# Putting the row of maxima in place with five products and a copy instead of a transpose and a transfer, for the first twelve heads

## The chip, the cores and the metric

The kernel runs on one core of a Trainium2 chip. The metric is the device time of one execution in microseconds (us). The core has five engines with queues of their own: TensorE (PE in the profile; its weight loads are PEld), VectorE (DVE), ScalarE (ACT), GpSimd (POOL) and SyncE (SP). Transfers between memories go through 16 DMA engines; SP, POOL and ScalarE issue them.

## The reference

```python
# q, k, v: (8, 8, 576, 64)   batch, heads, sequence, head size
scores = (1 / 8) * q @ k.transpose(0, 1, 3, 2)
scores = where(pos_i // 64 >= pos_j // 64, scores, -1e9)   # causal in blocks of 64
scores = scores - scores.max(-1, keepdims=True)
attn = exp(scores)
attn = attn / (attn.sum(-1, keepdims=True) + 1e-9)
x = (attn @ v).transpose(0, 2, 1, 3).reshape(4608, 512)
h = x @ moe_w_in                                           # 512 x 2048
sp = maximum(h, 0) + log1p(exp(-abs(h)))
out = (h * erf(sp)) @ moe_w_out                            # 2048 x 512
```

An attention over 64 heads (8 batches of 8) is followed by a dense layer with a gate ("MoE" in the names). The factors of the inputs make the scores large, so that the maximum must be subtracted. The weights come in as 64-bit numbers.

## The kernel before, in words

**Heads.** The head number n runs from 0 to 63 in one loop. In turn n the program writes out together: the load of a later head (`load_qk`), the maxima of head n + 2 (`maxes`), the probabilities of head n (`probs`), the products with v of an earlier pair (`pv`), the normalising of a group of four heads (`normalise`), the conversion of raw weights (`conv`, `split_next`; lines 130 to 136 and 156 to 157) and steps of the dense layer (`moe1`). Each is a list of steps with a start and an end between 0 and 1, and `merge` interleaves the lists by these numbers. The Tile framework then plans the order in which each engine gets the instructions, from their costs, their dependencies and this order of writing. An engine works through its queue in order.

**A head's tile.** `qk_of(n)` is a tile of 128 partitions with four parts of 576 columns: `klh`, `qhl`, `kh`, `qh`. Partitions 0 to 63 of `kh` and `qh` hold the high part of k and q (float32 rounded to a shorter form), and `klh` and `qhl` hold residuals and copies with which the product becomes more exact. Five more partitions of `kh` and `qh`, 64 to 68 (`D` to `D + 4`, with D = 64), are extra rows of the product: four mask rows, which put a large negative number on the half of a diagonal block that is masked, and one row that is 1 in `kh` and the row of maxima, with its sign turned, in `qh`. The product over 69 partitions then gives scores with the mask and with the maximum subtracted. Before the change the mask rows stand on partitions 64 to 67 and the constant row with the maxima on 68.

**Where the tiles lie.** Heads below EARLY = 12 go round through six tiles (four `qk`, two `qke`), later heads through four (NB = 4, NE = 2). The two others become weight slots after head 12. The rows of `maskrows` are put into the six tiles once, at the start. Head n + 4 is loaded in turn n below 12, head n + 3 above 12: POOL issues two loads (lines 408 and 410, or 412 and 414), SP one (`st`), and later POOL computes the residuals (lines 417 and 420). Early heads get part of their copies from ScalarE (line 427).

**Maxima.** In `maxes(n)`, steps a to d multiply the queries of a head by its keys (line 444, tile `s`, over 68 partitions: q, k and the mask rows) and VectorE takes the negated maximum of each row of scores into a column of `mx`, 128 queries by five columns (line 447). Step e joins the last two columns (line 472). Then the maxima, which lie one per partition, must become one row of 576 numbers on one partition of `qh`. Before: one transpose of `mx[:, :5]` (line 474) gives five partitions of 128 numbers in PSUM, ScalarE copies them to `mt` (line 476), and a transfer issued on ScalarE's queue writes the five pieces one after the other to partition 68 (line 477).

**Probabilities.** `probs(n)` multiplies `kh` by `qh` over 69 partitions (line 490, tile `t`) and adds the residual product (line 491); ScalarE takes the exponential (line 495). The product of line 490 reads the row of maxima. The products with v are line 539 and the sums of rows line 562; for the first 24 heads both are in float32. `normalise` sends x to DRAM (`x_d`) through POOL (lines 626 and 627).

**PSUM.** `bank` gives out a PSUM bank for each product: before the dense layer has loaded its first x, seven banks in rotation, later four.

**Dense layer.** `moe1` multiplies x by w_in (line 201), applies the gate (lines 169 to 177, of which line 177, the residual `m_gl`, runs on POOL while heads are in work) and multiplies by w_out (line 210). It starts when the first batch of eight heads is normalised and the first weights are converted. After the last head only it is left.

Of the kernel before, what the change touches and what calls it, by code (L numbers as in the profile page):

```python
# [23 lines left out]
def f32(ap):  # L24
    return ap.bitcast(F32)
# [7 lines left out]
def tile_attention_moe(ctx: ExitStack, tc: tile.TileContext, qk, v, w, maskrows, selws, out):  # L33
    nc = tc.nc
    B, H, D4, S = qk.shape
    D = D4 // 4
    NT, DM = out.shape
    NF = w.shape[0]
    P = 128
# [22 lines left out]
    ident = cpool.tile([P, P], F32, name="ident")  # L62
# [3 lines left out]
    zeros = cpool.tile([P, 1], F32, name="zeros")  # L66
# [26 lines left out]
    EARLY = 12  # L93
    NE = 2
# [181 lines left out]
    NB = 4  # L276
# [3 lines left out]
    def qk_of(n):  # L280
        return qks[n % len(qks) if n < EARLY else n % NB]
# [28 lines left out]
    with tc.tile_pool(name="apool", bufs=2) as apool, tc.tile_pool(name="spool", bufs=1) as spool, \  # L310
# [6 lines left out]
        mxs = [spool.tile([P, 7], F32, name=f"mx{i}") for i in range(2)]  # L317
# [15 lines left out]
        def bank(name):  # L333

            turn.append(0)
            k = len(turn) % 8 if not loaded else 0
            if k in (2, 5):
                return ps_h.tile([P, 512], F32, tag="h", name=name)
            if k in (3,):
                return ps_o.tile([P, 512], F32, tag="o", name=name)  # L340
            return ps_a.tile([P, 512], F32, tag="a", name=name)
# [55 lines left out]
        def part(n, i):  # L397

            return qk_of(n)[:, i * S : (i + 1) * S]

        def load_qk(n):
            b, h = divmod(n, H)
            t = qk_of(n)[:, : 4 * S].rearrange("p (i n) -> p i n", n=S)
            st = apool.tile([P, S], F32, tag="st", name=f"st_{n}", bufs=2)

            def a():
                if n < COPIED:
                    nc.gpsimd.dma_start(t[:D, 2:4, :], qk[b, h, 2 * D :].rearrange("(s d) n -> d s n", d=D))
                    nc.sync.dma_start(st, qk[b, h, : 2 * D])
                    nc.gpsimd.dma_start(t[D:, 0, :], qk[b, h, :D])  # L410
                    return
                nc.gpsimd.dma_start(t[:D, 1:4, :], qk[b, h, D:].rearrange("(s d) n -> d s n", d=D))
                nc.sync.dma_start(st, qk[b, h, : 2 * D])
                nc.gpsimd.dma_start(t[D:, 0:2, :], qk[b, h, : 2 * D].rearrange("(s d) n -> d s n", d=D))

            def low_q():
                nc.gpsimd.tensor_tensor(out=t[D:, 1, :], in0=st[D:, :], in1=f32(t[D:, 1, :]), op=ALU.subtract)

            def c():
                nc.gpsimd.tensor_tensor(out=t[:D, 0, :], in0=st[:D, :], in1=f32(t[:D, 2, :]), op=ALU.subtract)  # L420
                if n >= COPIED:
                    low_q()

            def copies(mx):
                for r, src in ((slice(0, D), f32(t[:D, 3, :])), (slice(D, P), st[D:, :])):
                    nc.vector.tensor_copy(t[r, 1, :1][:1], mx[r, 0:1][:1])
                    nc.scalar.copy(t[r, 1, :], src)
                low_q()

            if n < COPIED:  # L430
                copied[n] = copies
            return a, c

        COPIED = EARLY
        copied = {}

        def maxes(n):

            mx, K = mxs[n % 2], D + 4
            kh, qh = part(n, 2), part(n, 3)  # L440

            def mm(dst, i, k0, w_):
                r = min(P, S - i * P)
                nc.tensor.matmul(dst[:r, :w_], lhsT=qh[:K, i * P : i * P + r], rhs=kh[:K, k0 : k0 + w_], start=True, stop=True)  # L444

            def red(col, src, r=P):
                nc.vector.tensor_reduce(out=mx[:r, col : col + 1], in_=src, axis=AX.X, op=ALU.max, negate=True)  # L447

            def a():
                s = bank(f"s01_{n}")  # L450
                mm(s, 0, 0, 256)
                mm(s[:, 256:], 1, 0, 256)
                red(0, s[:, :128])
                red(1, s[:, 256:])

            def b():
                s = bank(f"s2_{n}")
                mm(s, 2, 0, 384)
                red(2, s[:, :384])

            def c():
                s = bank(f"s3_{n}")
                mm(s, 3, 0, 512)
                red(3, s)

            def d(j):
                s = bank(f"s4_{n}_{j}")
                mm(s, 4, 288 * j, 288)
                red(5 + j, s[:64, :288], 64)

            def e():
                nc.vector.tensor_reduce(out=mx[:64, 4:5], in_=mx[:64, 5:7], axis=AX.X, op=ALU.min)
                pt = bank(f"mt{n}")
                nc.tensor.transpose(out=pt[:5, :P], in_=mx[:, :5], identity=ident)
                mt = apool.tile([5, P], F32R, tag="mt", name=f"mt_{n}")
                nc.scalar.copy(mt, pt[:5, :P])
                nc.scalar.dma_start(f32(qk_of(n)[D + 4 : D + 5, 3 * S : 4 * S + 64]).rearrange("o (i p) -> o i p", p=P), f32(mt))

            return [a, b, c, lambda: d(0), lambda: d(1), e]

# [173 lines left out]
        for n in range(2):  # L654
            *steps, rows[n] = maxes(n)
            for f in steps:
                f()
            copied.pop(n)(mxs[n])
            if n:
                copied.pop(2)(mxs[n])  # L660
            if n == 0:
                v32 = load_v(0, 0, mxs[0][:1, 3:4])
                rows.pop(0)()
            next_raw(mxs[n][:1, 3:4])
# [34 lines left out]
        for n in range(N + 3):  # L699
# [9 lines left out]
            if n + 2 < N:  # L709
                *steps, rows[n + 2] = maxes(n + 2)  # L710
                lists.append((late("max", steps), 0, 1))
# [16 lines left out]
            if n % 2 == 0 and 2 <= n <= N:  # L728
                j = n // 2 - 1
# [75 lines left out]
```

## Time and profile before

| | |
|---|---|
| time, median of 3 runs | 1230.59 us (1229.72 to 1231.5) |
| profiled execution | 1236.01 us, span 1234.2 us |
| TensorE busy | 1149.7 us, 93% of the span |
| VectorE, ScalarE busy | 825.6 us (67%), 863.8 us (70%) |
| POOL busy | 476.2 us (39%) |
| mean granted TensorE clock | 0.973 |
| bytes moved by DMA | 148.24 MB, mean 120 GB/s |

How to read it: the span is one execution between its first and its last instruction. A row of a group has line, engine, operation, the tile written <- the tiles read, shapes and count; behind the first bar the busy time and the mean of one in ns, behind the second the idle time of the engine just before these instructions and what ended it. In a timeline a row has start, duration, engine, line and operation, and in brackets the idle time before it with what ended it. A waits row has the waiting engine, tile and line <- what it waited for: us in total, times, longest. `qke` is one of the two tiles that exist only for the early heads. PEclk is the clock that TensorE was granted, as a share of the full one.

### The profile page before, as it was taken

To read this page: it belongs to the slowest core of one execution; us is meant where nothing else is said; L and a number is where in the kernel's file an instruction comes from. 1 tells how busy PE (TensorE), PEld (TensorE's weight loads), DVE (VectorE), ACT (ScalarE), POOL (GpSimd) and SP (SyncE) were. 2 spreads that over 40 slices of the span, in tenths; PEclk is the share of its full clock that TensorE was granted. 3 is DMA by queue.
4 is the path that set the end of the run, shared out by engine and by line. 5 is a ranking of instruction groups with operands and counts; after the bars stand their busy time and mean duration, and the time that the engine had idled before them with its cause. 6 is when DMAs were issued, how large, how long until landed. Compare 5 with 4: busy or idle time off the path is not lost.

```text
span 1234.2 us, 23125 instructions
## 1 busy us (share of the span) xinstructions
PE 1149.7 (93%) x8874; PEld 795.7 (64%) x8874; DVE 825.6 (67%) x1559; ACT 863.8 (70%) x1675; POOL 476.2 (39%) x459
## 2 busy tenths in 40 slices
PE   6878988889999999999999999999999999999996
PEld 3555655666666667767766676766766766666663
DVE  5888887795676767677668666666667644555454
ACT  3675866686676776777777776777867776766664
POOL 7556154534353434435454444435443312100000
PEclk9886999999998999999999999999999999999999
DMA  9796368544554445453453445444544121121202
GB/s 235 215 248 172 115 192 215 145 100 110 128 139 109 120 118 123 129 140 100 122 139 93 128 110 129 107 127 110 121 113 117 56 63 61 62 69 52 69 26 77
DMA packets 94111, 148.24 MB, mean 120 GB/s; under 512 B 7620, under 2 KB 44804, under 8 KB 94002
## 3 DMA queue, kind: packets, MB, share of 16 engines
q1 hardware_dynamic: 69696, 93.34, 25.0%
q0 software_dynamic: 23616, 53.15, 20.3%
q8 instruction: 70, 1.15, 0.4%
q10 hardware_dynamic: 690, 0.28, 0.1%
q14 instruction: 39, 0.32, 0.1%
HBM read 118.15 MB, written 28.31 MB: 119 GB/s over the span
## 4 chain that ended last, share of the span: by engine, by line
PE 34%; DVE 27%; ACT 26%; DMA 6%; issue 6%; POOL 1%; ACTq 0%; DVEq 0%; SPq 0%; POOLq 0%
PE m_h L201 11%; PE o L210 10%; DVE m_r L173 6%; DVE m_r L174 6%; DVE m_r L175 5%; PE u L539 5%; ACT m_r L170 4%; ACT m_r L169 4%; ACT m_r L172 4%; ACT m_r L171 4%; ACT m_gh L176 3%; DVE mx L447 3%; PE t L490 2%; PE s L444 2%; PE t L491 2%
## 5 line engine op out<-in xcount | busy, mean ns | idle before, releaser
L201 PE MATMUL m_h<-xh,w 128*128 128x256 f16 x1584 | 323.6, 274 | 7.9 <-DVE m_r L175 7.1
L201 PEld LDWEIGHTS <-w 128*128 128x128 f16 x2376 | 224.4, 98 | 97.3 <-issue 10.2
L177 POOL TENSOR_TENSOR m_gl<-m_r,m_gh 128x512 f16<-128x512 f32 x114 | 135.9, 1192 | 290.3 <-ACT m_gh L176 265.5
L210 PE MATMUL o<-w,m_gh 128*128 128x512 f16 x792 | 233.7, 383 | 1.1 <-DVE pt L252 1.1
L447 DVE TENSOR_REDUCE mx<-s 64x1 f32<-64x288 f32 (+4 forms) x384 | 173.7, 469 | 88.5 <-PE s L444 87.7
L173 DVE SCALAR_TENSOR_TENSOR m_r<-m_r,m_r 128x512 f32<-128x512 f32 x144 | 118.7, 824 | 168.8 <-ACT m_r L172 164.2
L176 ACT CAST m_gh<-m_r 128x512 f16<-128x512 f32 x144 | 88.8, 617 | 182.8 <-DVE m_r L175 181.8
L201 PE MATMUL m_h<-xl,w 128*128 128x256 f16 x792 | 216.7, 274 | 0.0
L495 ACT ACTIVATE p<-t 128x288 f32<-128x288 f32 (+4 forms) x384 | 143.4, 382 | 60.7 <-PE t L491 52.2
L490 PE MATMUL t<-qk 69*128 69x288 f32 (+1 forms) x360 | 158.6, 442 | 17.2 <-DMA qk<-mt 9.5
L444 PE MATMUL s<-qk 68*128 68x256 f32 (+2 forms) x360 | 141.2, 426 | 17.3 <-DMA qk<-qk 8.4
L201 PE MATMUL m_h<-xh,we 128*128 128x256 f16 x720 | 149.1, 276 | 6.1 <-DVE m_r L175 5.9
L210 PE MATMUL o<-w,m_gl 128*128 128x512 f16 x396 | 143.4, 385 | 0.0
L169 ACT ACTIVATE m_r<-m_h,c,bs 128x512 f32<-128x512 f32 (+3 forms) x192 | 123.9, 665 | 27.2 <-PE m_h L201 23.9
L210 PEld LDWEIGHTS <-m_gh 128*128 128x128 f16 x1152 | 100.7, 98 | 63.4 <-issue 9.6
L201 PEld LDWEIGHTS <-we 128*128 128x128 f16 x1080 | 102.6, 99 | 50.2 <-issue 9.4
L420 POOL TENSOR_TENSOR qk<-st,qk 64x576 fp32r<-64x576 f32 x60 | 87.3, 1455 | 107.4 <-DMA qk<-qk 89.3
L507 DVE TENSOR_TENSOR p<-p,p 128x832 f16<-128x832 f32 x80 | 81.5, 1019 | 65.8 <-ACT p L506 65.6
L174 DVE SCALAR_TENSOR_TENSOR m_r<-m_r 128x512 f32<-128x512 f32 x144 | 119.0, 826 | 3.2
L491 PE MATMUL t<-qk 128*128 128x288 f32 (+1 forms) x360 | 112.8, 314 | 0.0
L210 PE MATMUL o<-we,m_gh 128*128 128x512 f16 x360 | 103.8, 385 | 5.2 <-ACT m_gh L176 5.2
L171 ACT ACTIVATE m_r<-m_r,c 128x512 f32<-128x512 f32 x144 | 103.7, 720 | 2.7 <-ACT m_r L170 0.6
(141 smaller groups left out, 1953.0 us busy)
## 6 DMA issues: line engine op xcount, KB each, us to landing
qk<-qk POOLq DMA_DIRECT2D x52, 432.0 KB, 4.8
st<-qk SPq DMA_DIRECT2D x64, 288.0 KB
qk<-qk POOLq DMA_DIRECT2D x60, 288.0 KB, 4.9
raw<-w SPq DMA_DIRECT2D x32, 512.0 KB
v<-v SPq DMA_DIRECT2D x16, 640.0 KB
x_d<-xs POOLq DMA_DIRECT2D x32, 288.0 KB, 3.2
xh<-x_d SPq DMA_DIRECT2D x36, 256.0 KB
xl<-x_d SPq DMA_DIRECT2D x36, 256.0 KB
```

The source lines that it names most:

```text
L169: nc.scalar.activation(r0s[:, :, lo:hi], h[:, :, lo:hi], AF.Tanh, bias=const(p1), scale=bss[b][g][:, 0:1])
L171: nc.scalar.activation(r0, r1, AF.Square, bias=const(b2), scale=a2)
L173: nc.vector.scalar_tensor_tensor(out=r0, in0=r0, scalar=c4, in1=r1, op0=ALU.add, op1=ALU.mult)
L174: nc.vector.scalar_tensor_tensor(out=r0, in0=r0, scalar=c5, in1=r0, op0=ALU.add, op1=ALU.mult)
L177: (nc.gpsimd if lag[-1] == 3 else nc.vector).tensor_tensor(out=gl, in0=r0, in1=gh, op=ALU.subtract)
L201: nc.tensor.matmul(h[:, k, :], lhsT=wf[:, a, sl], rhs=x[:, cc, :], start=cc == 0 and i == 0, stop=cc == NCC - 1 and i == 2)
L210: nc.tensor.matmul(o[c], lhsT=a[:, sl], rhs=wf[:, b_, :], start=u == u0 and k == 0 and not lo and b_ == 2, stop=u == u1 - 1 and k == nu - ...
L444: nc.tensor.matmul(dst[:r, :w_], lhsT=qh[:K, i * P : i * P + r], rhs=kh[:K, k0 : k0 + w_], start=True, stop=True)
L447: nc.vector.tensor_reduce(out=mx[:r, col : col + 1], in_=src, axis=AX.X, op=ALU.max, negate=True)
L490: nc.tensor.matmul(s[:kk, :w_], lhsT=kh[:K, ks], rhs=qh[:K, q0 : q0 + w_], start=True, stop=False)
L491: nc.tensor.matmul(s[:kk, :w_], lhsT=klh[:, ks], rhs=qhl[:, q0 : q0 + w_], start=False, stop=True)
L495: nc.scalar.activation(p32s[part][:kk, c : c + w_ - skip], s[:kk, skip:w_], AF.Exp, scale=SCALE)
```

## The change

For heads below 12, step e of `maxes` makes five products with the identity instead of one transpose. Each has one column of `mx` as its stationary operand and writes 128 numbers to partition 64 of a PSUM bank: four into one bank, the fifth into a second. ScalarE copies the first 512 numbers and then the last 64 from there straight into `qh`, on the same partition 64. The transfer is gone for these heads. For later heads the transpose, the copy and the transfer stay; only the partition written to is now 64.

For this the rows change places: the constant row and the row of maxima move to partition 64, the mask rows to 65 to 68. The products for the maxima (line 444) must read the mask rows, so they now read 69 partitions, and the row of maxima of the head that had the tile before would be in them. So, from the seventh head on (n >= 6), POOL writes zeros to partition 64 of `qh` before it issues the head's loads.

```diff
@@ load_qk
             def a():
+                if n >= NB + NE:
+                    nc.gpsimd.tensor_copy(t[D : D + 1, 3, :], zeros[D : D + 1].broadcast_to([1, S]))
                 if n < COPIED:
@@ maxes
-            mx, K = mxs[n % 2], D + 4
+            mx, K = mxs[n % 2], D + 5
...
             def e():
                 nc.vector.tensor_reduce(out=mx[:64, 4:5], in_=mx[:64, 5:7], axis=AX.X, op=ALU.min)
+                if n < EARLY:
+                    for c, w_ in ((0, 4), (4, 1)):
+                        pt = bank(f"mt{n}_{c}")
+                        for i in range(w_):
+                            nc.tensor.matmul(pt[D : D + 1, i * P : (i + 1) * P], lhsT=mx[:, c + i : c + i + 1], rhs=ident, start=True, stop=True)
+                        q0, q1 = c * P, min(S, (c + w_) * P)
+                        nc.scalar.copy(qh[D : D + 1, q0:q1], pt[D : D + 1, : q1 - q0])
+                    return
                 pt = bank(f"mt{n}")
                 nc.tensor.transpose(out=pt[:5, :P], in_=mx[:, :5], identity=ident)
                 mt = apool.tile([5, P], F32R, tag="mt", name=f"mt_{n}")
                 nc.scalar.copy(mt, pt[:5, :P])
-                nc.scalar.dma_start(f32(qk_of(n)[D + 4 : D + 5, 3 * S : 4 * S + 64]).rearrange("o (i p) -> o i p", p=P), f32(mt))
+                nc.scalar.dma_start(f32(qk_of(n)[D : D + 1, 3 * S : 4 * S + 64]).rearrange("o (i p) -> o i p", p=P), f32(mt))
@@ kernel
     for j in range(4):
-        maskrows[j, 1, 128 * j : 128 * j + 64] = -(2.0**100)
-        maskrows[j, 0, 128 * j + 64 : 128 * j + 128] = 1.0
-    maskrows[4, 0] = 1.0
+        maskrows[j + 1, 1, 128 * j : 128 * j + 64] = -(2.0**100)
+        maskrows[j + 1, 0, 128 * j + 64 : 128 * j + 128] = 1.0
+    maskrows[0, 0] = 1.0
```

## The prediction

> **What bounds the kernel now.** I read the page's head and its forty slices first, to see which engine is full in which stage.
>
> ```profile
> span 1234.2 us, 23125 instructions
> PE 1149.7 (93%) x8874; PEld 795.7 (64%) x8874; DVE 825.6 (67%) x1559; ACT 863.8 (70%) x1675; POOL 476.2 (39%) x459
> PE   6878988889999999999999999999999999999996
> PEclk9886999999998999999999999999999999999999
> ```
>
> TensorE is 93% busy over the whole, and from the sixth slice on nearly full at an almost full clock. Only the first four or five slices of 30.9 us have holes and a low clock. The twelve heads that the change names lie there, so I cut that stage into tens of microseconds.
>
> ```profile
> core 0: us, PE busy (x) PEld busy (x) DVE busy (x) ACT busy (x) POOL busy (x), PEclk, DMA share, GB/s
> 20.00:30.00 10.00, 6.67 (x33) 5.09 (x34) 6.33 (x17) 6.35 (x17) 5.31 (x6) 0.88 0.91 281
> 30.00:40.00 10.00, 9.13 (x48) 6.07 (x47) 5.63 (x14) 6.66 (x15) 7.62 (x7) 0.60 0.91 246
> 40.00:50.00 10.00, 8.11 (x67) 5.70 (x66) 9.80 (x25) 7.24 (x22) 6.79 (x7) 1.00 0.54 139
> 60.00:70.00 10.00, 8.02 (x57) 5.73 (x48) 9.74 (x26) 8.10 (x22) 4.89 (x5) 0.84 0.93 240
> 80.00:90.00 10.00, 5.85 (x44) 3.83 (x37) 7.42 (x22) 8.38 (x23) 4.41 (x5) 0.96 0.90 248
> 90.00:100.00 10.00, 10.00 (x75) 6.62 (x73) 4.92 (x10) 4.38 (x11) 4.38 (x4) 0.70 0.83 167
> ```
>
> No single engine holds this stage. From 20 to 40 us the DMA engines are full (share 0.91); from 40 to 80 VectorE is (9.80 and 9.74 of 10); from 80 to 100 neither is: TensorE first sits idle, then works at a clock of 0.70. Next: what TensorE waits for up to 130 us, and where.
>
> ```profile
> PE t L490 <- DMA qk<-mt: 9.5, 6, 3.1
> PE t L490 <- DMA qke<-mt: 1.1, 1, 1.1
> ...
> 27.12 0.37 PE L490 MATMUL t<-qk 69*128 69x288 f32 x1 [3.08 <-DMA qk<-mt]
> ...
> 81.64 0.37 PE L490 MATMUL t<-qk 69*128 69x288 f32 x1 [1.02 <-DMA qk<-mt]
> 89.26 0.58 PE L490 MATMUL t<-qk 69*128 69x288 f32 x1 [3.13 <-DMA qk<-mt]
> ```
>
> The transfer of the row of maxima (`qk<-mt`) ends seven waits of TensorE, 10.6 us together, two of them over 3 us. The chain of work that ended last, cut to 12 to 130 us, tells which of them count.
>
> ```profile
> by line: PE u L539 12.6%; DMA qk<-mt 12.5%; DMA raw<-w 11.3%; DVE mx L447 8.0%; issue 6.7%; DVE w L133 5.7%; PE t L490 5.3%; DVE w L132 3.9%; PE s L444 3.6%; PE t L491 3.1%; ACT p L495 2.8%; DVE w L157 2.5%; DMA st<-qk 2.3%; ACT w L156 2.3%
> ...
> 13.18 6.93 DMA qk<-mt
> 31.72 6.86 DMA raw<-w
> 49.39 6.49 DMA raw<-w
> 77.86 3.64 DMA qk<-mt
> 84.93 4.20 DMA qk<-mt
> 90.98 4.88 PE u L539 x20
> 144.73 3.00 PE u L539 x28
> ```
>
> 12.5% of 118 us is 14.8 us: three transfers of the row (6.93, 3.64, 4.20). The 3.08 us wait before 27.12 is not among them: there the chain goes through the loads of raw weights. The last two rows are for the clock. The same products of line 539 took 4.88 us for twenty right after the 3.13 us hole, 244 ns each, and 3.00 us for twenty-eight later, 107 ns each.
>
> **The change part by part.** These are the groups whose durations I use:
>
> ```profile
> L474 PE MATMUL mt<-ident,mx x12: 272/274/421, 12.4 to 121.0; 128*5 128x128 f32 x12
> L474 PE MATMUL mt<-ident,mx x4: 272/274/275, 46.8 to 77.3; 128*5 128x128 f32 x4
> 148.07 0.27 PE L474 MATMUL mt<-ident,mx 128*5 128x128 f32 x1
> 148.18 0.59 PE L210 MATMUL o<-w,m_gh 128*128 128x512 f16 x2
> L539 PE MATMUL u<-p,v 128*64 128x128 f32 x48 | 6.1, 317 | 0.0
> L476 ACT CAST mt<-mt 5x128 fp32r<-5x128 f32 x64 | 15.8, 247 | 7.8 <-PE mt L474 7.0
> L477 ACTq DMA_DIRECT2D qk<-mt x9: 699/700/720, 13.2 to 135.9; - x9
> L176 ACT CAST m_gh<-m_r 128x512 f16<-128x512 f32 x144 | 88.8, 617 | 182.8 <-DVE m_r L175 181.8
> L495 ACT ACTIVATE p<-t 64x64 f32<-64x64 f32 x64 | 13.4, 209 | 11.9 <-PE t L491 10.7 <-PE s L444 0.8 <-ACT a L130 0.2
> L328 POOL CAST selw<-zeros x1: 613/613/613, 18.9 to 18.9; 128x512 fp32r<-128x512 f32 x1
> ```
>
> *Removed, in each of twelve heads:* one transpose, one ScalarE copy of 247 ns, one transfer. The transpose lasts 274 ns but holds TensorE for little: the next matmul started 0.11 us after it (148.07 to 148.18). The transfer's issue holds ScalarE's queue for up to 0.70 us.
>
> *Added on TensorE:* five plain f32 products of one column of maxima with the 128 columns of the identity. No row shows such a product alone. From below: 107 ns, the mean step of the f32 stream of line 539. From above: 317 ns, the full duration of a 128-column f32 product of line 539. I take 0.21, the middle, because the five follow each other, so their ends overlap, but they all go to one PSUM partition, so I do not expect them side by side as in that stream. Then a head costs 5 x 0.21 - 0.11 = 0.94 us more on TensorE (bounds 0.43 and 1.48), twelve heads 11.3 us (5 to 18).
>
> *Where this lies on the path:* the twelve transposes run from 12.4 to 121.0 us, four of them between 46.8 and 77.3. Up to 70 us the pace is set by loads and VectorE, and TensorE has the holes quoted; I cost the seven heads there at nothing. If that cover goes, they cost 6.6 us. Five heads (the one at 77.3 us and the four after it) run where the chain passes through TensorE: 5 x 0.94 = 4.7 us.
>
> *Added on ScalarE:* a copy of 1x512 and one of 1x64, by the rows of 128x512 (617 ns) and 64x64 (209 ns) 0.83 us, less the 0.25 of the old copy: +0.58 us a head. Against it the queue is free of a 0.70 us issue, so I cost it at nothing; bounds -0.1 and +0.58 us a head. A new wait comes with it: the second copy sits in ScalarE's queue until the fifth product is done, and the exponentials of line 495 and the weight conversions stand behind it. That is one product more, 0.2 to 0.3 us, which ScalarE's idle time (a sixth to a third in the windows above, up to 90 us) covers.
>
> *The row's latency:* instead of 3.6 to 6.9 us of transfer there are four more products (0.84) and about 0.6 us more of copying, some 1.4 us. The first product of `t` (288 columns) needs only the first copy.
>
> *What the removed waits give, one by one:*
> ```profile
> 19.87 0.68 ACT L130 ACTIVATE a<-raw 128x512 f32<-128x512 f32 x1 [2.71 <-DMA raw<-w]
> 21.71 0.68 DVE L132 SCALAR_TENSOR_TENSOR w<-a,w 128x512 int32<-128x512 int32 x1
> ```
> - The first (13.18 to 20.11): next on the chain is VectorE's weight conversion, begun at 21.71. It needs line 130, which began at 19.87 when its own load landed, so it can begin at 20.55: 1.2 us gained, not 6.9. Late next: the raw weights.
> - Before 27.12: not on the chain, but the clock was 0.60 in the ten microseconds from 30. I take 0.5; bounds 0, and 3.1 with 9.13 x 0.4 = 3.7 for the clock.
> - Before 81.64: 1.0 us.
> - Before 89.26: 3.1 us of idle. I keep all of it, since the extra products were charged above. And if the hole is short the clock stays up: twenty products at 107 instead of 244 ns save 2.7 us. Together 5.8.
> - The four small waits lie under a full VectorE or full DMA: nothing.
> Sum 8.5 us; at most 17.0 (10.6 of waits, 2.7 and 3.7 of clock).
>
> *Added on POOL:* from the seventh head on, a write of zeros on one partition of 576 elements ahead of the head's loads, 0.66 us by the 613 ns of 512 elements; 58 of them, 38 us on an engine that is 39% busy.
>
> ```profile
> L412 POOL DMA_DIRECT2D qk<-qk x52 | 33.4, 643 | 113.7 <-PE t L491 88.3 <-PE o L210 12.7 <-PE s L444 7.9
> PE s L444 <- DMA qk<-qk: 8.4, 3, 7.0
> L444 PE MATMUL s<-qk 68*128 68x256 f32 (+2 forms) x360 | 141.2, 426 | 17.3 <-DMA qk<-qk 8.4
> 300.00:400.00 100.00, 95.84 (x753) 66.74 (x753) 64.87 (x118) 66.91 (x129) 41.01 (x39) 0.97 0.48 120
> ```
>
> It waits for the matmuls that last read this slot, as the load behind it does already (88.3 us). Queued behind it are two load issues, the residuals of lines 420 and 417, MoE's subtraction of line 177, and the x residuals. All come up to 0.66 us later. The second row counts TensorE's waits for loads of q and k up to 130 us, 8.4 us in three places, and the third, over the whole span, has no more. I cost it at nothing; bounds: 0, and 0.66 us for each of 52 late heads, 34 us, if the loads became the pace. In the steady stage TensorE has four percent idle (95.84 of 100), which no part of the change touches.
>
> *Moved:* the row of maxima and the constant row exchange places with the mask rows, and the maxima's matmul reads 69 rows instead of 68. The shape of its moving columns stays: nothing. One PSUM bank more is drawn for each early head, from seven in rotation: within the range.
>
> *The sum:* 8.5 - 4.7 = 3.8 us. The profiled execution took 1236.0 us, span 1234.2; the median of the runs is 1230.6, so this execution is 0.4% long, and I take the difference off the median: 1226.8.
>
> **A rule against it.** The Trainium skill, "TensorE: Matmul & The Clock Gate", section Terms, says that the transpose mode is four times faster for FP32. By that rule a plain product steps at 4 x 0.11 = 0.44 us, which is the price of the second rival below. The trace has no lone plain f32 product to settle it; the stream of line 539 (107 ns) speaks against it, but its products may run side by side.
>
> **The rivals.** About 0.2%, 2.5 us, is what a measurement of this kernel can tell from no change.
>
> *Hidden anyway (no change).* The wait goes but its time goes elsewhere: TensorE reaches `t` earlier and finds ScalarE behind with exponentials, or the raw weights not landed, or the copy of the row stuck in ScalarE's queue, so that `t` still waits for it. For it: a full VectorE from 40 to 80 us, and the two raw loads of 6.86 and 6.49 us on the chain. Against it: the stretch from 80 to 100 us, where VectorE, ScalarE and TensorE all have holes. Then the last gain shrinks from 5.8 to about 3, the others to 1.7, against 4.7 of products: 1230.6.
>
> *The products are dear (slower).* They step at 0.44 us, four times the transpose's step; a low clock alone would bring them there, since 0.21 x 244 / 107 is 0.48. A head then costs 5 x 0.44 - 0.11 = 2.1 us more. Five heads on the path: 10.5. The three heads from 46.8 us to before 77.3 no longer fit beside VectorE, since TensorE is 8 of 10 busy there: 6.3. Less 8.5: 8.3 slower, 1238.9. It decides from the price at which five heads eat 8.5 us: (8.5 / 5 + 0.11) / 5 = 0.36 us a product.
>
> *POOL's zeros delay the late heads (slower).* A tenth of the 34 us would eat the gain, and two fifths (13.6) give 1240. Against it: no TensorE wait for those loads after 130 us.
>
> **How the numbers follow.** Forecast 0.46, own range 1219 to 1228; hidden 0.28, 1228.1 to 1233.1; dear products 0.19; zeros 0.07. So faster by over 0.2% 0.46, within 0.28, slower 0.26. All bounds at once reach from 1216 (17.0 gained, 0.43 x 5 paid) to 1248 (nothing gained, 1.48 x 12 paid). I cut to 1219 to 1236, which leaves out the dearest products and the deepest gains, about 2 in 10.
>
> **What would show it.** In the changed kernel's trace: five matmuls of `mt` in each of twelve heads with steps near 0.2 us (0.4: the rival); no wait of TensorE on `DMA qk<-mt` in that stage; instead short waits on ScalarE's copy, under 10.6 us in all; a clock above 0.7 from 90 to 100 us; the first MoE products of line 201 some 4 us earlier; line 177 and the loads as before with 58 casts of some 0.66 us on POOL, and no TensorE wait on loads after 130 us. I am wrong if TensorE's holes up to 130 us stay the same length under another name, or if the order on the engines, which is planned anew from the changed instructions, opens holes elsewhere.

## The result, and the profile after

The changed kernel takes 1248.93 us (median of 4 runs, 1246.32 to 1250.21) against 1231.05 before: 1.46% slower, 95% interval 1.29% to 1.63%. I had forecast 1226.8 and a range up to 1236.

The page of the changed kernel, its head and its slices:

```profile
span 1247.3 us, 23466 instructions
PE 1168.8 (94%) x8982; PEld 800.3 (64%) x8982; DVE 835.2 (67%) x1559; ACT 872.2 (70%) x1687; POOL 527.3 (42%) x517
PE   7988998799999999999999999999989999999997
PEclk8888899999999999999999999999999999999999
PE 35%; ACT 25%; DVE 24%; DMA 6%; issue 6%; POOL 3%; ACTq 0%; DVEq 0%; SPq 0%; POOLq 0%
```

TensorE is busier by 19 us and no less full: its idle time went from 84.5 to 78.5 us, and the time still rose. Of the 19 us, 16.5 are the new products: 20.2 us of matmuls into `mt` up to 140 us, where the twelve transposes had 3.7. On an engine that is 94% busy that looks like the whole loss; the runs below speak against it. POOL has 51 us more and 3% of the chain instead of 1%.

What TensorE waits for in the changed kernel up to 140 us (in total, times, longest):

```profile
PE s L446 <- DMA qk<-qk: 7.2, 2, 6.6
PE t L500 <- DVE mx L449: 2.2, 1, 2.2
PE mt L479 <- DVE v L349: 2.1, 1, 2.1
...
PE t L500 <- ACT qke L481: 1.0, 1, 1.0
```

The seven waits of 10.6 us on the row's transfer are gone, and waits of `t` on the copy that replaces it are 1.0 us. So the change does what it says. The matmuls issued in the first two stretches of 130 us show what came of that. First the kernel before, then the changed one:

```profile
0.00:130.00 130.00, 101.03 (x613) 66.64 (x614) 97.54 (x241) 80.62 (x193) 79.25 (x97) 0.83 0.83 217
130.00:260.00 130.00, 116.54 (x867) 78.74 (x865) 105.89 (x212) 91.21 (x209) 57.12 (x51) 0.97 0.60 161
```

```profile
0.00:130.00 130.00, 109.61 (x640) 64.49 (x640) 95.01 (x218) 79.29 (x187) 87.08 (x102) 0.86 0.75 198
130.00:260.00 130.00, 112.57 (x815) 74.44 (x813) 98.03 (x193) 87.27 (x199) 57.84 (x55) 0.93 0.60 160
```

TensorE (first column) is 8.6 us busier up to 130 us, but 108 of its matmuls are the extra ones: each f32 product shows as two records, so twelve heads have 120 instead of 12. Without them the changed kernel has issued 1347 matmuls by 260 us, against 1480: it is 133 behind. A matmul between 130 and 260 us takes 116.5 / 867 = 0.134 us on the mean, so it is some 18 us behind. That it is also 17.9 us slower by the medians is partly chance: the two executions shown here differ by 13.1 us in span, because the profiled one of before was a long one. Up to 130 us the share of the DMA engines (last but one) fell from 0.83 to 0.75: the loads come later. The dense layer's first product (line 201) shows the same; before, then after:

```profile
L201 PE MATMUL m_h<-xh,w x75: 272/273/421, 126.1 to 159.9; 128*128 128x256 f16 x75
```

```profile
L201 PE MATMUL m_h<-xh,w x56: 269/273/437, 137.6 to 156.6; 128*128 128x256 f16 x56
```

It starts 11.5 us later. The chain of the changed kernel, in the stretch ahead of that start:

```profile
100.91 7.77 DMA st<-qk
108.82 3.47 POOL qk L422
112.37 1.40 POOL qk L419
113.77 0.81 POOL qk L408
114.58 1.31 POOL qke L419
115.89 5.85 DMA qk<-qk
121.80 1.41 POOL qk L422
...
126.17 1.20 POOL qk L408
...
128.05 2.52 POOL xs L636 x2
130.57 0.70 POOL x_d L637
131.26 3.42 DMA x_d<-xs
```

From 100 to 135 us the chain runs through transfers and POOL, apart from some 3 us put down to issue. Two writes of zeros (line 408) stand in it, 2.0 us together, ahead of a load and of the x that the dense layer waits for. In the kernel before, the chain runs mostly through TensorE, VectorE and ScalarE there. At the start of the kernel ScalarE shows another new wait. Before:

```profile
10.40 0.67 ACT L427 CAST qk<-qk 64x576 fp32r<-64x576 f32 x1
```

After:

```profile
14.58 0.58 ACT L481 CAST qk<-mt 1x512 fp32r<-1x512 f32 x1
15.18 0.67 ACT L429 CAST qk<-qk 64x576 fp32r<-64x576 f32 x1
...
16.70 1.40 POOL L419 TENSOR_TENSOR qk<-st,qk 64x576 fp32r<-64x576 f32 x1 [5.09 <-ACT qk L481]
```

The copy of the first row now stands ahead of the copies of q in ScalarE's queue; they begin at 15.18 instead of 10.40 us, and POOL waits 5.09 us.

### The profile page after: what moved, and what is told of

It reads as the page before. It is cut to its first block, busy times and chain, and to the rows that moved or that the text cites. A ratio compares the mean times of both kernels' runs of the same rounds, so it can differ in the third digit from the quotient of the medians.

```text
span 1247.3 us, 23466 instructions
## 1 busy us (share of the span) xinstructions
PE 1168.8 (94%) x8982; PEld 800.3 (64%) x8982; DVE 835.2 (67%) x1559; ACT 872.2 (70%) x1687; POOL 527.3 (42%) x517
## 4 chain that ended last, share of the span: by engine, by line
PE 35%; ACT 25%; DVE 24%; DMA 6%; issue 6%; POOL 3%; ACTq 0%; DVEq 0%; SPq 0%; POOLq 0%
PE m_h L201 11%; PE o L210 10%; DVE m_r L173 6%; DVE m_r L174 5%; DVE m_r L175 4%; ACT m_r L170 4%; ACT m_r L169 4%; ACT m_r L172 4%; ACT m_r L171 4%; PE u L549 4%; ACT m_gh L176 3%; PE t L500 2%; PE s L446 2%; PE t L501 2%; DVE mx L449 2%
## 5 line engine op out<-in xcount | busy, mean ns | idle before, releaser
L201 PE MATMUL m_h<-xh,w 128*128 128x256 f16 x1584 | 325.9, 275 | 10.6 <-DVE m_r L175 7.9
L500 PE MATMUL t<-qk 69*128 69x288 f32 (+1 forms) x360 | 157.7, 438 | 10.6 <-DVE mx L449 7.8
L446 PE MATMUL s<-qk 69*128 69x256 f32 (+1 forms) x360 | 141.3, 424 | 15.6 <-DMA qk<-qk 7.2
```

What stands on the lines that cost most here:

```text
L201: nc.tensor.matmul(h[:, k, :], lhsT=wf[:, a, sl], rhs=x[:, cc, :], start=cc == 0 and i == 0, stop=cc == NCC - 1 and i == 2)
L500: nc.tensor.matmul(s[:kk, :w_], lhsT=kh[:K, ks], rhs=qh[:K, q0 : q0 + w_], start=True, stop=False)
```

## The experiments

The theories: A, the loss lies in products and copies; B, it lies in POOL's zeros, by their time (B1) or by the new waits (B2); C, it lies in the order, which is planned anew when instructions change. D, about ScalarE's queue, is told at its run. Ratios are to the kernel before, run beside it on the same chip, where its median was 1228 to 1231 us; behind each ratio stands its 95% interval. Longer edits are shown in part.

**No products** (exchange of rows and zeros stay):

```diff
-                if n < EARLY:
+                if n < 0:
                     for c, w_ in ((0, 4), (4, 1)):
```

> The changed kernel without its products: all 64 heads get their row by transpose, copy and transfer, as before. The exchange of rows, the 69 partitions and POOL's 58 writes of zeros stay. Theory A (the loss of 18 us sits in the products, the copies and their places in the queues up to the twelfth head): close to the kernel before, 1231 to 1236. Theory B (POOL's zeros and the later loads cost it): 1241 to 1249. Theory C (any change of instructions deals the order anew, and the old order was a lucky one): also above 1238, but then with holes that are not next to POOL's zeros.

1243.2 us, 1.15% slower (0.56 to 1.74). So, by the middle value, most of the loss comes without a single product. Its two stretches:

```profile
0.00:130.00 130.00, 99.28 (x580) 64.87 (x580) 97.51 (x232) 77.96 (x187) 89.25 (x107) 0.80 0.80 213
130.00:260.00 130.00, 113.67 (x805) 76.35 (x804) 96.34 (x187) 85.20 (x197) 55.36 (x52) 0.92 0.55 150
```

It loses 33 matmuls up to 130 us and 62 after. My prediction had looked for this cost in waits of TensorE on loads, and there are no more of them than before (8.6 us in three places up to 140 us, against 8.4, and none later); the loss shows in what is issued.

**No zeros** (products and copies stay; the maxima's product reads the old row):

```diff
-                if n >= NB + NE:
-                    nc.gpsimd.tensor_copy(t[D : D + 1, 3, :], zeros[D : D + 1].broadcast_to([1, S]))
```

> The changed kernel without the writes of zeros on POOL, so that the product for the maxima of a head reads the row of the head that had the tile before; products and copies stay. Theory A: 1243 to 1249, the delay of 10 us at the twelfth head stays and only the 3 to 4 us that grow later go. Theory B: 1231 to 1237.

1240.25 us, 1.01% slower (0.25 to 1.78).

```profile
0.00:130.00 130.00, 111.97 (x642) 64.89 (x642) 92.22 (x218) 79.06 (x188) 78.20 (x93) 0.89 0.76 199
130.00:260.00 130.00, 116.48 (x863) 79.20 (x864) 105.38 (x212) 92.53 (x211) 58.02 (x53) 0.95 0.65 172
```

Less 108 extra ones, it is 79 matmuls behind at 130 us and loses 4 more by 260. So the products' half loses its time before 130 us, the zeros' half mostly after. Each alone costs about 1%, together 1.46%. By the middle values they do not add up, but the two intervals are wide enough that they might.

**Every product twice:**

```diff
                             nc.tensor.matmul(pt[D : D + 1, i * P : (i + 1) * P], lhsT=mx[:, c + i : c + i + 1], rhs=ident, start=True, stop=True)
+                            nc.tensor.matmul(pt[D : D + 1, i * P : (i + 1) * P], lhsT=mx[:, c + i : c + i + 1], rhs=ident, start=True, stop=True)
```

> The changed kernel with each of the sixty products issued twice into the same place. One product steps at 0.236 us at full clock in the trace of the changed kernel (ten records in 1.18 us) and 0.46 us at half clock, so 14 to 28 us of TensorE are added. If TensorE's time for the products is what was lost: 1259 to 1272. If it is covered and only their place in the queues counts: 1249 to 1253.

1249.05 us, 1.70% (1.06 to 2.34), against the change's 1.46% (1.29 to 1.63). In its trace the matmuls into `mt` have 35.9 us instead of 20.2. Of these 15.7 us the time shows 0.24%, 3 us, give or take 8, so most of them are covered here. A cost of some 5 us would not stand out.

**Products from the third head on:**

```diff
-                if n < EARLY:
+                if 2 <= n < EARLY:
```

> The changed kernel, but heads 0 and 1 get their row by transpose, copy and transfer; heads 2 to 11 by products. In the changed kernel the first copy of a row stands in ScalarE's queue ahead of the copies of q with which the heads start, and those start at 15.2 instead of 10.4 us. If this start is a large part of the loss: 1241 to 1245. If not: 1247 to 1251.

1250.2 us, 1.78% (1.18 to 2.38). The late copies of q at the start, plain as they are in the trace, are not what sets the end.

**Zeros that nobody reads,** in the kernel before:

```diff
             def a():
+                if n >= NB + NE:
+                    nc.gpsimd.tensor_copy(t[96:97, 3, :], zeros[96:97].broadcast_to([1, S]))
```

> The kernel before, with POOL's 58 writes of zeros added in the same places but to partition 96 of the tile, which nothing reads: the same 38 us of POOL, no wait for the matmuls of the head before, nobody waits for them. Theory B1 (POOL's time, in order ahead of the loads, is the cost): about as slow as the run without products, 1.0 to 1.3% over before. Theory B2 (the cost is the new dependence: zeros wait for the last matmul of the slot, the maxima's products wait for the zeros): within 0.3% of before.

1244.11 us, 1.27% (0.91 to 1.62). This run is not the clean one that I meant: with nothing to wait for, the writes were planned into the first 130 us, where POOL goes from 79.25 to 106.94 us of work:

```profile
0.00:130.00 130.00, 96.66 (x531) 61.62 (x531) 93.27 (x216) 73.01 (x177) 106.94 (x135) 0.79 0.75 197
```

It shows that such writes can cost 1% without a wait for the matmuls. But the other engines' order is not quite the old one either, so POOL's time and the new order are not told apart, and it does not show what the writes cost at the places of the change.

**Zeros on VectorE,** without products:

```diff
-                    nc.gpsimd.tensor_copy(t[D : D + 1, 3, :], zeros[D : D + 1].broadcast_to([1, S]))
+                    nc.vector.tensor_copy(t[D : D + 1, 3, :], zeros[D : D + 1].broadcast_to([1, S]))
```

> The run without products (all rows by transfer, rows exchanged), with the zeros written by VectorE instead of POOL. B1: the cost goes from POOL; what is left is at most 58 short VectorE writes of about 0.4 us, mostly covered after 130 us: 0 to 0.4% over before. B2: unchanged, 1.0 to 1.3% over before.

1240.88 us, 0.82% (0.56 to 1.08): between the two theories. Freed of POOL, most of the loss stays.

**Ten zeros instead of 58,** with the products:

```diff
-                if n >= NB + NE:
+                if NB + NE <= n < EARLY + NB:
...
-                nc.scalar.dma_start(f32(qk_of(n)[D : D + 1, 3 * S : 4 * S + 64]).rearrange("o (i p) -> o i p", p=P), f32(mt))
+                nc.scalar.dma_start(f32(qk_of(n)[D + 5 : D + 6, 3 * S : 4 * S + 64]).rearrange("o (i p) -> o i p", p=P), f32(mt))
```

> The whole change, but late heads get their row on partition 69, which has a constant row of its own, so that partition 64 must be cleared only for heads 6 to 15: 10 writes instead of 58. If the zeros cost where POOL and the loads are the pace, up to about 260 us: 5 to 8 us of the loss stay for them, 1.2 to 1.5% over before in all. If every write costs alike: 48 of 58 parts of the loss by zeros go, about 0.9% over before, as in the run without zeros.

1241.84 us, 1.18% (0.66 to 1.69). The interval holds both answers.

**From the third head, no zeros:** the edits of the second and fourth run together.

> Products for heads 2 to 11 only, and no zeros written (the maxima's product of a head reads the row of the head before in its tile). The run without zeros lost 9.4 us by the third head and 13 by the sixth. If that start, where the row's copy stands ahead of the copies of q on ScalarE, is the products' loss: within 0.4% of before. If the loss comes from products and copies of later heads: still 0.8 to 1.0% over before.

1241.55 us, 1.03% (0.66 to 1.40): as without zeros. The start is ruled out a second time.

By now each edit cost about 1%, and no term of mine said why. The next runs keep the old order, or change nothing but the order.

**Exchange only:** products and zeros both out.

> The change without products and without zeros: only the rows are exchanged and the maxima's product reads 69 partitions, one of them the row of the head that had the tile before (its output leaves out the clearing). Its instructions stand in the same order as the kernel before's on all engines. All theories: within 0.2% of before. If it is slower, the 69th partition or the place of the transfer costs something that I have not seen.

1230.57 us, 0.11% (-0.12 to 0.33). The exchange and the 69th partition cost nothing that can be measured here. In the traces of this run and the next two, every engine's instructions do stand in the order of the kernel before, apart from the added writes. In the run without products, which has the full writes, the order of POOL, VectorE and TensorE is another one.

**Writes of one element,** on top of that:

```diff
                 if n >= NB + NE:
-                    nc.gpsimd.tensor_copy(t[D : D + 1, 3, :], zeros[D : D + 1].broadcast_to([1, S]))
+                    nc.gpsimd.tensor_copy(t[D : D + 1, 3, :1], zeros[D : D + 1])
```

> As the run above, with POOL's 58 writes at the same places and with the same dependences, but of one element instead of 576 (it leaves out the rest of the clearing). The order of all other engines is again that of the kernel before, and POOL's too apart from the 58 insertions. Theory C (what is lost is the old order, dealt anew by any added work): within 0.3% of before. Theory B2 (the waits that the writes add cost it): 0.8 to 1.2% over before. Theory B1 (POOL's time): within 0.3%, since 58 short writes are some 5 us of POOL.

1230.99 us, 0.17% (-0.05 to 0.38). So the waits that these writes add cost nothing that can be measured. But they are not the same waits as those of the full writes. Element 0 of the row is read by the first of a head's products of line 500 alone (the others read columns that start later), so the short write waits for that first product, and the full one for the last that reads the row. POOL sat idle for 3.5 us ahead of these writes until such a product was done, against 11.7 us in the run without products. B2 falls for the early wait only; for the later one it stays open.

**Four such writes:**

```diff
-                    nc.gpsimd.tensor_copy(t[D : D + 1, 3, :1], zeros[D : D + 1])
+                    for i in range(4):
+                        nc.gpsimd.tensor_copy(t[D : D + 1, 3, i : i + 1], zeros[D : D + 1])
```

> As the run with writes of one element, but four such writes in a row at each of the 58 places: 4 x 0.18 = 0.72 us by the trace of that run, as much of POOL as one write of 576 elements (0.66 us), and again the old order on all engines. Theory B1 (POOL's time ahead of the loads): 0.8 to 1.2% over before, like the run without products. Theory C (the order): within 0.3% of before.

1236.23 us, 0.59% (0.30 to 0.89), between the two theories. POOL's time by itself, in the old order and with the early waits, costs some 0.4% more than the single small write (0.59 - 0.17, give or take 0.4). Rows of the write in three kernels, the changed one, the one with one element, and this one (56 of the 58 places; the other two write to `qke`):

```profile
L408 POOL CAST qk<-zeros x56: 656/659/3057, 29.4 to 965.1; 1x576 fp32r<-1x576 f32 x56
```

```profile
L408 POOL CAST qk<-zeros x56: 178/180/919, 21.6 to 938.4; 1x1 fp32r<-1x1 f32 x56
```

```profile
L409 POOL CAST qk<-zeros x224: 177/178/1263, 23.2 to 936.1; 1x1 fp32r<-1x1 f32 x112
```

The median of 659 ns is what I had priced (0.66 us). The error was to count it at nothing.

**Two other orders of the kernel before,** with no work added:

```diff
-                lists.append((late("max", [rows.pop(n + 1)]), 0, 0.6))
+                lists.append((late("max", [rows.pop(n + 1)]), 0, 0.7))
```

> The kernel before with the same instructions in another order: the end of the stretch in which a row of maxima may be placed goes from 0.6 to 0.7 of a turn. 96% of ScalarE's and 97% of VectorE's instructions keep their relative order. Theory C: 0.5 to 1.2% over before, with no work added. Theories A and B: within 0.3%.

1232.0 us, 0.27% (0.06 to 0.48): less than theory C expected.

```diff
-                lists.append((late("prob", probs(n, prs[n])), 0, 1))
+                lists.append((late("prob", probs(n, prs[n])), 0.02, 1))
```

> The kernel before with the same instructions, in an order changed more: the probabilities of a head begin at 0.02 of the turn instead of 0. 85% of ScalarE's and 87% of VectorE's instructions keep their relative order. Theory C: 0.5 to 1.5% over before. Theories A and B: within 0.3%.

1234.92 us, 0.67% (0.35 to 0.99). An order alone can cost half a per cent.

**Copies of the row on VectorE,** no zeros:

```diff
-                        nc.scalar.copy(qh[D : D + 1, q0:q1], pt[D : D + 1, : q1 - q0])
+                        nc.vector.tensor_copy(qh[D : D + 1, q0:q1], pt[D : D + 1, : q1 - q0])
```

> The run without zeros, with the two copies of the row on VectorE instead of ScalarE. Theory D (ScalarE's queue: copies of the row stand there ahead of the copies of q and the exponentials): under 0.5% over before. Theory C: still 0.5 to 1.2% over, as any new order; VectorE is the fuller engine from 40 to 130 us, so more is possible.

1238.58 us, 0.78% (0.47 to 1.09). Taking the copies off ScalarE does not bring the time back; theory D is not borne out.

**The run without zeros in two other orders,** the row's stretch ended at 0.3 and at 1.0 instead of 0.6:

```diff
-                lists.append((late("max", [rows.pop(n + 1)]), 0, 0.6))
+                lists.append((late("max", [rows.pop(n + 1)]), 0, 0.3))
```

> The run without zeros, with the stretch of a turn in which a row may be placed ended at 0.3 instead of 0.6: same work, another order. Theory C: anything from 0.2 to 1.6% over before; the spread between this run, the next and the run without zeros (1.0%) is then what an order is worth. If products and copies cost the time in themselves: 0.9 to 1.1% over before, in all three.

1231.68 us, 0.21% (-0.09 to 0.51).

> The run without zeros, with that stretch ended at 1.0. As for the run before this one: 0.2 to 1.6% by theory C, 0.9 to 1.1% if the products and copies cost it in themselves.

1240.56 us, 0.95% (0.63 to 1.28). The same products and copies, in place of the same transfers, cost 0.2, 0.8, 1.0 or 1.0%, by the order and the engine of the copy. So they have no net cost of their own that reaches 1%. The two stretches of the run with 0.3:

```profile
0.00:130.00 130.00, 106.18 (x673) 64.61 (x675) 100.85 (x228) 83.56 (x197) 82.50 (x97) 0.89 0.81 212
130.00:260.00 130.00, 119.49 (x899) 80.84 (x891) 109.75 (x224) 95.08 (x215) 58.12 (x51) 0.97 0.61 161
```

The loads keep their share (0.81), and by 260 us it is only 16 matmuls behind the kernel before. Yet with every transfer of a row gone for twelve heads it is not faster either. TensorE's idle time up to 130 us falls from 29.0 to 23.8 us only, although 10.6 us of waits went, and the products have 22.1 us of TensorE where the transposes had 3.7. TensorE's longest waits in it up to 130 us, of which the second, third and fifth are new:

```profile
PE s L444 <- DMA qk<-qk: 7.9, 2, 6.5
PE s L444 <- DVE mx L472: 5.1, 2, 4.2
PE mt L477 <- ACT rs L573: 2.4, 1, 2.4
PE wt L143 <- DVE wrs L141: 1.8, 1, 1.8
PE mt L477 <- ACT p L503: 1.2, 1, 1.2
```

**The change in that order:** the same edit of the stretch on the whole change.

> The change as it is, with its 58 writes of zeros, and rows of maxima placed up to 0.3 of a turn instead of 0.6. If the order cost about 0.8% of the loss and POOL's writes 0.6%: 0.6 to 1.0% over before. If the zeros cost their full 1.15% in any order: 1.2 to 1.5%.

1243.08 us, 1.18% (0.75 to 1.60). Against the run with 0.3 and no zeros, the zeros cost about 1% again (1.18 - 0.21, give or take 0.5).

**A form without repeated clearing,** in that order; the main lines, against the changed kernel (the products, the transfers of later heads and the 33 mask rows follow suit):

```diff
-            mx, K = mxs[n % 2], D + 5
+            mx, K = mxs[n % 2], D + 4
...
-            K = D + 5
+            K = 97
...
-                        nc.scalar.copy(qh[D : D + 1, q0:q1], pt[D : D + 1, : q1 - q0])
+                        nc.scalar.copy(qh[96:97, q0:q1], pt[96:97, : q1 - q0])
...
-        masks = [qks[n][D : D + 5, 2 * S : 4 * S] for n in range(NB + NE)]
+        masks = [qks[n][D : D + 33, 2 * S : 4 * S] for n in range(NB + NE)]
```

> The whole computation with products and copies for twelve heads and no repeated clearing: constant row and row of maxima on partition 96, mask rows on 64 to 67 as before, the rows between cleared once at the start by larger transfers of the mask rows (33 instead of 5, 0.76 MB more, 2 to 4 us of early DMA), the maxima's product over 68 partitions; rows of maxima placed up to 0.3 of a turn. The order is that of e15 but for the start. Theory C with the zeros' own cost: as e15 and the early DMA, 0.2 to 0.6% over before. If the row's wait were worth what I forecast, it would be 0.3% faster than before.

1233.7 us, 0.41% slower (0.16 to 0.65). By the two ratios it is some 13 us better than the change as made, and still slower than the kernel before. No version that I ran beats the kernel before.

## Why the prediction was wrong, point by point

I forecast 3.8 us gained and measured 17.9 lost. Three steps failed: POOL's zeros, put at nothing, cost 0.5 to 1.2%; the gain of 8.5 us less 4.7 for the products came out as a loss in every order tried, of 2.6 us in the best (or none, by its interval); and the new order, to which I gave no price, is worth 0.3 to 0.8% by itself.

**The waits that go.** They went, all 10.6 us, and from 90 to 100 us the clock was 1.00 instead of 0.70, as I had hoped. The step that failed is the sum of what they give and what replaces them: 8.5 - 4.7 = 3.8 us gained, by forecast. The best order, the run at 0.3 without zeros, measured 2.6 us lost (0.21%, -0.09 to 0.51). I had taken each wait by itself and kept everything else in its place. With the transfer gone the instructions stand in another order, other waits end last in the same stage, and TensorE's holes turn into work that does not advance the dense layer: its first product came 11.5 us later in the changed kernel, not 4 earlier. No run removes the transfers without adding products, so how much of the error is the 8.5 and how much the 4.7 stays open.

**The products.** At full clock (granted 1.00) a product took 0.236 us, ten records in 1.18 us, against my 0.21. At half clock (0.50) eight records took 1.85 us, 0.46 us a product. Here they are, in the changed kernel:

```profile
39.91 1.18 PE mt L479 x10
71.48 1.85 PE mt L479 x8
```

That 0.21 is so near is luck. It lies between 107 and 317 ns, which are figures of one matmul record, and I read them as those of a product; the f32 products of line 539 show as two records each as well, so a product of that stream took 214 ns. And the full clock was not there for all: over the sixty the trace has 20.2 us, 0.34 us each, between my price and the rival's. The 4.7 us on the path are neither shown nor refuted, since the run with doubled products leaves room for them. As the cause of the loss the dear products fall: 1.15% is lost without any product, and with all sixty the best order loses 0.2%. The rule of the Trainium skill that stood beside that rival ("TensorE: Matmul & The Clock Gate", Terms, four times for FP32) would have them at 0.44 us; at full clock this trace has 0.236, about twice the transpose's 0.11.

**POOL's zeros.** I cost them at nothing because POOL is 39% busy and TensorE does not wait for loads after 130 us; the rival that they delay the heads got 0.07. Added to the exchange they cost 1.15%, to the products at 0.3 they cost 0.97%, and to the products in the change's own order 0.45%, the last with an interval as wide as itself. About 0.4 to 0.6% is POOL's time in the old order. The rest, by difference only, is the new order or the full write's later wait; the two were not told apart. The share of busy time was the wrong measure: in the chain from 100 to 135 us POOL and transfers take turns with some 3 us between them.

**The new order.** I named it in the last sentence, and gave it neither a price nor a chance. It was the large unknown: with the same work 0.3 and 0.7% for the kernel before, and 0.2 to 1.0% for the products. The orders that I tried were all slower than the old one or equal to it. I did not show which single place in an order costs the time. The first product of the dense layer, or the matmuls issued by 260 us, show a loss as it arises, but not what is left of it: the form on partition 96 is 73 matmuls behind by 260 us, some 10 us, and only 5 us slower in the end.

**ScalarE at nothing** and **the exchange at nothing**: the second is shown (0.11%). The first is not refuted: moving the copies off ScalarE gained nothing clear, though ScalarE's copies waited 6.4 us for the products up to 140 us, where they had waited 2.6 for the transposes.

**The bounds.** The 1248 us that I called all bounds at once left out the 34 us that I had named for POOL and the copies' 0.58 us a head, and the measured 1248.93 lies just beyond it. The range up to 1236 also left out both slower rivals, at 1238.9 and 1240, to which I gave 0.26 together.

**The bound of 0.2%.** One run of the kernel before lies between 1220 and 1237 us, so that twelve runs tell the ratio to 0.2 or 0.3% either way, and four runs to 0.2 to 0.8%.

## What to carry to other kernels

Where a planner orders the queues, an edit's cost is its own work plus a new order, and the second can be the larger: measure an edit in two or three orders, and look for a form of it that keeps the old order, as the one-element writes did here, and check that it keeps the waits too, which they did not. A wait is worth what the stage gains without it, not its length: ask what ends last there next, loads and in-order queues included. A short instruction ahead of a load on an engine that is 40% busy need not be free: four writes of 0.18 us instead of one, at 58 places, cost some 0.4% here with the order unchanged. In which stage was not shown.

## What the runs showed of the hardware

A plain f32 product of 128 columns shows as two matmul records, 120 for the sixty here, and an f32 transpose as one, 12 for twelve. A write on POOL took 0.18 us for one element and 0.66 us for 576, and once 3.06 us. 384 products over 69 partitions instead of 68 cost nothing that can be measured (0.11%, -0.12 to 0.33).
